# Gate products and last products of a gated unit as seven block products per pair of batches, with the operand places in another order

## The chip, the cores and the metric

The kernel runs on one core of one Trainium2 chip. The time is device microseconds of that core; each version is run several times, and its time is the median. The engines are PE (TensorE, matrix products), DVE (VectorE), ACT (ScalarE), POOL (GpSimd) and SP (SyncE, which starts the transfers). They run side by side, each through its own list of instructions, and wait for each other by semaphores. SBUF is the on-chip memory of 128 partitions; PSUM is the memory that PE writes, here eight banks of one result tile each.

## The reference

Attention, a mixing unit and a gated unit follow each other, all in float32, for 4 batches of 448 tokens and 768 features:

```
attn  = causal softmax(q k^T / 8) v                 # 4 batches, 12 heads, 448 tokens, 64 wide
x     = attn as [4, 448, 768]
u     = x + (relu(x^T w_tok1) w_tok2)^T             # over tokens, 448 -> 256 -> 448
u     = u + relu(u w_ch1) w_ch2                     # over features, 768 -> 1536 -> 768
h     = relu(u w_in)                                # 768 -> 1024
a, v  = h[..., :512], h[..., 512:]                  # gates, values
vn    = (v - mean(v)) / sqrt(var(v) + 1e-6)         # over the 512 features
vs    = w_spatial vn + b_spatial                    # over the 448 tokens
out   = (a * vs) w_out                              # 512 -> 768
```

## The kernel before

Every float32 operand x of a product is split into a high part (x rounded, written by ACT, `nc.scalar.copy`) and a low part (x minus the high part, written by DVE or POOL, `lo_part`), and a product takes three matmuls: high by high, high by low, low by high (`mm3`, lines L252 to L254). In names, `fb` and `fa` are such split factors of operands and weights, `whl` and `uhl` the same for plain products, `ghl` for the gated tiles, `gx` and `nhl` for normed values, `wv` for the value weights. A tile of the activations is feature-major: 128 features by 448 tokens; U0 to U3 hold the activations of the four batches.

The work: attention by pairs of heads (24 pairs), token mixing, then the mixing unit over features. Batches 0 and 1 take it by plain products (`channel`), batches 2 and 3 together (`channel_pair`): the two batches and two halves of the features make a matrix of two by two blocks, and so do the weights, and seven products of sums and differences of blocks stand for eight (`factors` and `weight_factors` make them, `seven` runs them; results `psf`, gathered into `hs` or added to U). Then the gated unit, batch by batch (`gate`): gate products (`psg`, 18 matmuls a tile, 4 tiles a batch), value products (`psv`, 18 matmuls of 512 columns), ACT's relu into one of two buffers `p0`, `p1`, the norm on DVE (L1141 to L1155, with a root on ACT between), spatial products (`psp`, 11 matmuls), on DVE the bias added and the gate multiplied, split into `ghl`, and the last products (`pso`, 12 matmuls a tile, 6 tiles a batch), copied to `gate` tiles and sent out.

All of this is declared as jobs of a planner (`Plan`) with priorities, what they read and write, and planned durations; it sets the order on each engine before the program is built, and gives each result the free bank of PSUM that became free last. Places in SBUF have names ("X", "A0", "h0", "st0", "P0") and are used one after another by different buffers. `EAGER, START, STEP` place the attention pairs in time.

## Time and profile before

| | us |
|---|---|
| median of 3 runs | 788.7 (788.41 to 789.03) |
| profiled execution | 789.54 |
| its span, first to last instruction | 787.8 |
| PE busy | 759.3 |
| PE weight loads busy | 651.9 |
| DVE busy | 541.5 |
| ACT busy | 394.7 |
| POOL busy | 314.0 |

The table gives the time in which each engine had an instruction under way. Matmuls overlap each other, so PE's busy time counts stretches and not the sum of the single durations. By the trace, the channel pair starts at about 416 us and the gated unit at about 562 us; the spatial products begin at about 690 us.

### The profile page before, as it was taken

The page shows a single profiled execution, that of the slowest core. Times are in us where ns is not written, and L with a number is a line of the kernel's source. Part 1 is how long each engine was busy: PE and PEld are TensorE (multiplying, and loading weights), DVE is VectorE, ACT ScalarE, POOL GpSimd, SP SyncE. Part 2 cuts the span into 40 slices and gives each one's busy share as a digit, 9 for nine tenths or more (in the row PEclk, how much of TensorE's full clock was granted, in tenths as well). Part 3 has the DMA queues.
Part 4 walks back from the last instruction along what each step waited for, and adds up shares of the span by engine and source line. Part 5 has one row for each costly group of instructions (what it writes and reads, how often), then busy time and mean ns, then how long its engine had stood idle before and what let it go on. Part 6 is the DMA issues. An engine that isn't in the chain of part 4 may idle for free.

```text
span 787.8 us, 12362 instructions
## 1 busy us (share of the span) xinstructions
PE 759.3 (96%) x4272; PEld 651.9 (83%) x4272; DVE 541.5 (69%) x1354; ACT 394.7 (50%) x977; POOL 314.0 (40%) x385
## 2 busy tenths in 40 slices
PE   5889899999999999999998999999999999999998
PEld 3467678788988788888897999989898898889997
DVE  5899888787777876775799679999601514383341
ACT  5999775627455664422445667453734323232110
POOL 4789645448766555643400000001797313031000
PEclk9999999999999999999999999999999999999999
DMA  7676687696857989888641221422321000001112
GB/s 260 216 239 235 210 296 237 222 350 225 290 163 224 302 282 284 255 261 267 195 151 41 85 78 39 156 105 74 101 88 48 1 1 0 1 1 70 71 47 93
DMA packets 49102, 123.32 MB, mean 157 GB/s; under 512 B 4880, under 2 KB 20368, under 8 KB 48528
## 3 DMA queue, kind: packets, MB, share of 16 engines
q1 hardware_dynamic: 49040, 122.54, 47.1%
q8 instruction: 33, 0.54, 0.3%
q14 instruction: 29, 0.24, 0.1%
HBM read 91.72 MB, written 30.80 MB: 156 GB/s over the span
## 4 chain that ended last, share of the span: by engine, by line
PE 71%; DVE 18%; ACT 5%; issue 2%; POOL 1%; DMA 1%; DVEq 0%; POOLq 0%; ACTq 0%
PE ps L252 7%; PE ps L254 7%; PE ps L253 7%; PE pss L400 4%; PE psf L252 4%; PE psf L253 4%; PE psf L254 4%; DVE fb L243 3%; PE pst L479 3%; PE pso L252 3%; PE pso L253 2%; PE pso L254 2%; PE psv L254 2%; PE psv L252 2%; PE psv L253 2%; PE psg L252 2%
## 5 line engine op out<-in xcount | busy, mean ns | idle before, releaser
L243 POOL TENSOR_TENSOR whl<-whl 128x768 fp32r<-128x768 f32 x45 | 83.7, 1862 | 82.5 <-ACT whl L718 81.4
L425 ACT ACTIVATE P<-P,stats 128x448 f32<-128x448 f32 (+1 forms) x192 | 95.9, 506 | 26.9 <-DVE stats L408 26.9
L442 POOL TENSOR_SCALAR P<-P,stats 128x448 f32<-128x448 f32 (+1 forms) x192 | 87.8, 477 | 51.2 <-DVE stats L434 34.0
L252 PE MATMUL psf<-fb,fa 128*128 128x448 f32 x252 | 93.2, 370 | 4.3 <-ACT uhl L724 1.7
L253 PE MATMUL psf<-fb,fa 128*128 128x448 f32 x252 | 92.9, 369 | 0.5 <-DVE fb L243 0.5
L254 PE MATMUL psf<-fb,fa 128*128 128x448 f32 x252 | 92.7, 368 | 0.0
L243 POOL TENSOR_TENSOR whl<-wf,whl 128x384 fp32r<-128x384 f32 x16 | 17.9, 1120 | 165.2 <-ACT whl L1054 165.2
L408 DVE CUSTOM_DVE_ANT_0 P<-pss,mask 128x448 f32<-128x448 f32 (+1 forms) x192 | 69.0, 412 | 14.1 <-PE pss L400 14.1
L1141 DVE BATCH_NORM_STATS2 bias<-v 128x6 f32<-128x512 f32 x14 | 9.7, 694 | 74.1 <-ACT v L1138 74.1
L855 ACT CAST fa<-raw 128x384 fp32r<-128x384 f32 x84 | 40.9, 511 | 39.0 <-PE psf L254 14.6
L718 ACT CAST whl<-whl 128x768 fp32r<-128x768 f32 x45 | 37.3, 832 | 43.9 <-DMA whl<-plain 41.9
L252 PEld LDWEIGHTS psf<-fb,fa 128*128 128x128 f32 x252 | 47.7, 189 | 10.4 <-issue 3.4
L252 PE MATMUL ps<-uhl,whl 128*128 128x448 f32 x144 | 55.0, 382 | 0.0
L252 PE MATMUL ps<-hid,whl 128*128 128x448 f32 x144 | 54.3, 377 | 0.4 <-DVE U L757 0.4
L254 PE MATMUL ps<-uhl,whl 128*128 128x448 f32 x144 | 52.8, 367 | 0.0
L254 PE MATMUL ps<-hid,whl 128*128 128x448 f32 x144 | 52.7, 366 | 0.0
L253 PE MATMUL ps<-uhl,whl 128*128 128x448 f32 x144 | 52.7, 366 | 0.0
L253 PE MATMUL ps<-hid,whl 128*128 128x448 f32 x144 | 52.7, 366 | 0.0
L253 PEld LDWEIGHTS psf<-fb,fa 128*128 128x128 f32 x252 | 47.8, 190 | 4.7 <-DVE fb L243 0.8
L243 DVE TENSOR_TENSOR fa<-raw,fa 128x384 fp32r<-128x384 f32 x84 | 46.8, 578 | 6.9 <-ACT fa L855 6.9
L254 PEld LDWEIGHTS psf<-fb,fa 128*128 128x128 f32 x252 | 47.8, 190 | 4.0
L243 POOL TENSOR_TENSOR uhl<-U,uhl 128x448 fp32r<-128x448 f32 x36 | 41.6, 1170 | 18.1 <-ACT uhl L1089 14.8
(175 smaller groups left out, 2037.4 us busy)
## 6 DMA issues: line engine op xcount, KB each, us to landing
way<-in_wch SPq DMA_DIRECT2D x24, 768.0 KB, 5.9
whl<-plain SPq DMA_DIRECT2D x45, 384.0 KB, 4.6
stage<-in_qkv SPq DMA_DIRECT2D x24, 448.0 KB, 4.6
plain<-way SPq DMA_DIRECT2D x24, 384.0 KB, 3.3
raw<-plain SPq DMA_DIRECT2D x24, 384.0 KB, 3.7
round<-PB SPq DMA_DIRECT2D x8, 1024.0 KB, 6.0
PT<-round SPq DMA_DIRECT2D x32, 256.0 KB, 6.2
v<-in_qkv SPq DMA_DIRECT2D x24, 256.0 KB, 3.5
```

The lines of the kernel that those rows point to most:

```text
L243: e.tensor_tensor(lo, x, hi.bitcast(F32), op=ALU.subtract)
L252: nc.tensor.matmul(ps, ah, bh, start=(first and i == 0), stop=False, **kw)
L253: nc.tensor.matmul(ps, ah, bl, start=False, stop=False, **kw)
L254: nc.tensor.matmul(ps, al, bh, start=False, stop=(last and i == n - 1), **kw)
L400: nc.tensor.matmul(ps(i, j), a.t[r, q0:q1], c.t[r, ks[j]], start=(k == 0), stop=(k == last))
L408: nc.vector.tensor_tensor_reduce(out=P(i)[:M, j, :], in0=ps(i, j), in1=mask[:M, S - 128 : S - 128 + W] if j == 0 and n < BLOCKS or M == 64 ...
L425: nc.scalar.activation(P(i)[:M, j, :], P(i)[:M, j, :], AF.Exp, bias=s.t[:M, 0, c : c + 1], scale=-1.0, accum_out=s.t[:M, 1, c : c + 1])
L442: nc.gpsimd.tensor_scalar(P(i)[:M, j, :], P(i)[:M, j, :], s.t[:M, 2, c : c + 1], 1.0, op0=ALU.mult, op1=ALU.mult)
L479: nc.tensor.transpose(ps.t[:, c : c + 128], src, ident)
L718: job("ACT", act(DM, False), lambda: nc.scalar.copy(w.t[:, 0, :], w.t[:, 1, :].bitcast(F32)), r=ks, w=ks, prio=p)
L855: nc.scalar.copy(w[o].t[:, z, 0], at(d))
L1141: nc.vector.bn_stats(sc(0, 6), v.t)
```

## The change

Gate products and last products are taken by pairs of batches (0 and 1, 2 and 3) as seven block products, like the channel pair. For a pair, `factors` makes the operand factors of the gate products from U, with an eighth place for the block b12, since the value products read the plain blocks of both batches; `gate_unit` makes the weight factors for one of two units; 252 instead of 288 matmuls. For the last products, the operand factors come from the gate tiles (`gated`), into which the spatial products now write, and the weight factors of all three units are made at once, 768 wide (`out_factors`); 252 instead of 288 matmuls, 6 to a block product. Results are gathered by ACT (copy, or activation) and by DVE (addition). Low parts of the gated unit's factors go to DVE (`GATE_DVE`, `OUT_DVE`, `NORMED_DVE`), the value weights stay with POOL and are loaded earlier, into other places. Further, the place X is two (X0, X1), `SETS` lists the places of the factors in another order, the first two factors of the channel pair have a higher priority (`EARLY`), and START and STEP are smaller.

```diff
-EAGER, START, STEP = 12, 115.0, 17.0
+EAGER, START, STEP = 12, 110.0, 16.7
...
+GATE_DVE = tuple(range(8))
+OUT_DVE = tuple(range(7))
...
+NORMED_DVE = (1, 2, 3)
+
+EARLY = 1e5 + 48
+VALUE_PRIO = -1e5 + 1.5
...
-    SETS = {2: ("h0", "h1", "h2"), 3: ("h3", "h4", "h5"), 4: ("qh0", "ql0", "qh1"), 5: ("A0", "A0", "v0"), 6: ("ql1", "st0", "st1"), 7: ("A1", "A1", "v1")}
...
+    SETS = (("qh0", "ql0", "qh1"), ("ql1", "st0", "st1"), ("A0", "A0", "v0"), ("A1", "A1", "v1"), ("h0", "h1", "h2"), ("h3", "h4", "h5"), ("X0",) * 3, ("X1",) * 3)
...
+    OVER = ((0, 0), (0, 0), (0, 1), (1, 0))
+
+    def factors(x, into, prio, place, on_dve=LO_DVE, early=None):
...
         def split(o, i, w):
             h, k, f = place[o][i]
             x_, wk = w
-            p = prio + 0.1 * o
+            p = (prio if early is None or o > 1 else early) + 0.1 * o
             job("ACT", act(S, False), lambda: nc.scalar.copy(f(0), x_()), r=wk, w=[(h, k, 0)], prio=p)
-            e, name, us = (nc.vector, "DVE", dve(S, False)) if o in LO_DVE else (nc.gpsimd, "POOL", pool(S))
+            e, name, us = (nc.vector, "DVE", dve(S, False)) if o in on_dve else (nc.gpsimd, "POOL", pool(S))
             job(name, us, lambda: lo_part(e, f(1), x_(), f(0)), r=[*wk, (h, k, 0)], w=[(h, k, 1)], prio=p, port=True)
...
-        for i in range(3):
+        for i in range(len(place[0])):
...
+            if len(place) > 7:
+                split(7, i, b12)
...
+    def split_weights(n, at, key, part, wkey, p, on_dve):
...
+        def split(o, d):
+            wk = wkey(o)
+            e, name, us_ = (nc.vector, "DVE", us) if o in on_dve else (nc.gpsimd, "POOL", pool(n))
+            job("ACT", act(n, False), lambda: nc.scalar.copy(part(o, 0), at(d)), r=[key(d)], w=[wk], prio=p + 0.1 * o)
+            job(name, us_, lambda: lo_part(e, part(o, 1), at(d), part(o, 0)), r=[key(d), wk], w=[wk], prio=p + 0.1 * o, port=True)
...
+    TO = ((0, 0), (0, 0), (1, 1), (0, 1), (0, 1), (1, 1), (1, 0))
+
+    def gather(o, ps, place, relu, prio):
+
+        h, hk = place(*TO[o])
+        if o in (0, 2, 3):
+            job("ACT", act(S), lambda: nc.scalar.copy(h(), ps.t[:, :S]), r=[(ps, 0)], w=hk, prio=prio)
+        elif o == 6:
+            job("ACT", act(S), lambda: nc.scalar.activation(h(), ps.t[:, :S], AF.Relu if relu else AF.Copy), r=[(ps, 0)], w=hk, prio=prio)
+        else:
+            job("DVE", dve(S), lambda: nc.vector.tensor_tensor(h(), ps.t[:, :S], h(), op=ALU.add), r=[*hk, (ps, 0)], w=hk, prio=prio)
+            if relu:
+                job("ACT", act(S, False), lambda: nc.scalar.activation(h(), h(), AF.Relu), r=hk, w=hk, prio=prio + 0.1)
...
+    def seven(us, place, base, done, start=()):
...
-                    mm3(ps.t[:, :S], [(w[o].t[:, z, 0, c], w[o].t[:, z, 1, c], place[o][i][2](0), place[o][i][2](1)) for i, c in enumerate((slice(0, 128), slice(128, 256), slice(256, 384)))], first=first, skip_group_check=True)
+                    w = us[z][0]
+                    mm3(ps.t[:, :S], [(w(o, 0, i), w(o, 1, i), place[o][i][2](0), place[o][i][2](1)) for i in range(n)], first=first, skip_group_check=True)
...
+                job("PE", 0.607 * n, mms, r=[*after, us[z][1](o), *((*place[o][i][:2], x) for i in range(n) for x in range(2))], w=[(ps, 0)], prio=base + 0.01 * o)
...
-            0,
+            places(*range(7)),
+            early=EARLY,
...
+        job("SP", 0.4, lambda k=k, w=w: nc.sync.dma_start(w.t, gated_w[8 + k]), r=[("gated", 8 + k)], w=[(w, 0)], prio=LOW + VALUE_PRIO + k, size=262144)
...
+        e, name, us = (nc.vector, "DVE", dve(FF, False)) if k in VALUE_DVE else (nc.gpsimd, "POOL", pool(FF))
+        job(name, us, lambda k=k, w=w, h=h, l=l, e=e: lo_part(e, l.t[:, k % 3, :], w.t, h.t[:, k % 3, :]), r=[(w, 0), (h, k, 0)], w=[(l, k, 1)], prio=LOW + VALUE_PRIO + k, port=True)
...
+    def gate_unit(f):
+
+        p = LOW + 110 + turn[0]
+        t, at, key = raw_blocks("w3", True)
+        for k in range(2):
+            for c in range(2):
+                job("SP", 0.4, lambda k=k, c=c: nc.sync.dma_start(t.t[:, k, c * HALF : c * HALF + HALF], gated_w[2 * f + 4 * k + c]), r=[("gated", 2 * f + 4 * k + c)], w=[(t, k, c)], prio=p, size=196608)
+        ws = [buf(tag, [2, 2, HALF], F32R, "fa") for tag in ("t0", "t1", "t2", "hid")]
+        split_weights(HALF, at, key, lambda o, x: ws[o // 2].t[:, o % 2, x], lambda o: (ws[o // 2], o % 2), p, GATE_DVE)
+        return lambda o, x, i: ws[o // 2].t[:, o % 2, x, 128 * i : 128 * i + 128], lambda o: (ws[o // 2], o % 2)
...
+    GATE_SETS = (5, 6, 7, 0, 1, 2, 3, 4), (6, 7, 0, 1, 5, 2, 3, 4)
...
+        place = factors(u_at, lambda k, i, u_at=u_at: u_at(*OVER[k], i), 1.0 + g, places(*GATE_SETS[g]), GATE_DVE)
+        dup = buf("e", [2, KM, 128], F32R, "xsh")
...
+        def hidden_pair(f, g=g, place=place):
+            if unit.get("f") != f:
+                unit.update(f=f, w=gate_unit(f))
+
+            def done(z, o, ps):
+                def at(r, x):
+                    h = gates[2 * g + x]
+                    return (lambda: h.t[:, 2 * r + f, :]), [(h, 2 * r + f)]
+
+                gather(o, ps, at, True, -1)
+
+            seven([unit["w"]], place, next_prio(), done)
+
+        if g == 0:
+            values(0)
+            hidden_pair(0)
+            values(1)
+            shared_values()
+            hidden_pair(1)
+        else:
+            hidden_pair(1)
+            values(0)
+            hidden_pair(0)
+            shared_values()
+            values(1)
...
+    gx = [buf(f"X{k}", [2, 2, FF], F32R, "gx") for k in range(2)]
...
+    def out_factors():
+
+        p0 = next_prio()
+        n = 2 * HALF
+        raws = [buf(f"A{k}", [2, n], F32, "raw") for k in range(2)]
+        more = buf("v1", [n], F32, "raw")
+        ws = [buf(t, [2, n], F32R, "fa") for t in ("hid", "t0", "t1", "t2", "P0", "P1", "x0")]
...
+        return [(lambda o, x, i, m=m: ws[o].t[:, x, HALF * i + 128 * m : HALF * i + 128 * m + 128], lambda o: (ws[o], 0)) for m in range(3)]
...
-            job("POOL", pool(FF), lambda c=c, x=x: lo_part(nc.gpsimd, ts[c - 1](1), x(), ts[c - 1](0)), r=[xk, tk[c - 1][0]], w=[tk[c - 1][1]], prio=p0)
+            e, name, us = (nc.vector, "DVE", dve(FF, False)) if c in NORMED_DVE else (nc.gpsimd, "POOL", pool(FF))
+            job(name, us, lambda c=c, x=x, e=e: lo_part(e, ts[c - 1](1), x(), ts[c - 1](0)), r=[xk, tk[c - 1][0]], w=[tk[c - 1][1]], prio=p0, port=True)
...
-            job("DVE", dve(S), lambda ps=ps, f=f: nc.vector.tensor_tensor(ps.t[:, :S], ps.t[:, :S], gates[b].t[:, f, :], op=ALU.mult), r=[p, (gates[b], f)], w=[p], prio=p0)
-            g = buf(("h0", "h1", "h2", "h3", "h4", "h5", "P0", "P1")[(4 * b + f) % 8], [2, S], F32R, "ghl")
-            job("ACT", act(S), lambda ps=ps, g=g: nc.scalar.copy(g.t[:, 0, :], ps.t[:, :S]), r=[p], w=[(g, 0)], prio=p0)
-            job("DVE", dve(S), lambda ps=ps, g=g: lo_part(nc.vector, g.t[:, 1, :], ps.t[:, :S], g.t[:, 0, :]), r=[p, (g, 0)], w=[(g, 1)], prio=p0)
...
+            job("DVE", dve(S), lambda ps=ps, f=f: nc.vector.tensor_tensor(gates[b].t[:, f, :], ps.t[:, :S], gates[b].t[:, f, :], op=ALU.mult), r=[p, gk], w=[gk], prio=p0)
...
+    def project(g, place, ws, units):
+        def done(z, o, ps):
+            def at(r, c):
+                i = 4 * (rows[0] + z) + 2 * r + c
+                h, k = gates[i % 8 // 2], 4 + i % 2
+                return (lambda: h.t[:, k, :]), [(h, k)]
+
+            gather(o, ps, at, False, -1)
+            if o in (1, 4, 5, 6):
+                (r, c), m = TO[o], units[z]
+                h, hk = at(r, c)
+                job("SP", 0.4, lambda: nc.sync.dma_start(out[2 * g + c, 128 * (m + 3 * r) : 128 * (m + 3 * r) + 128, :], h()), r=hk, prio=seq[0], size=229376)
+
+        seven([ws[m] for m in units], place, next_prio(), done)
+        rows[0] += len(units)
...
+    def gated(g, tags):
+        def at(r, c, i):
+            h = gates[2 * g + c]
+            return (lambda: h.t[:, 2 * r + i, :]), [(h, 2 * r + i)]
+
+        return factors(at, lambda k, i: at(*OVER[k], i), seq[0], pair_places(tags), OUT_DVE)
+
+    spatial(0, normed(0))
+    spatial(1, normed(1))
+    ws = out_factors()
+    place = gated(0, ("h0", "h1", "h2", "h3", "h4", "h5", "st0", "st1", "A0", "A0", "A1", "A1", "x1", "v1"))
+    spatial(2, normed(2))
+    project(0, place, ws, (0, 1))
+    ns = normed(3)
+    project(0, place, ws, (2,))
+    spatial(3, ns)
+    place = gated(1, ("X0", "X0", "X0", "X1", "X1", "X1", "w0", "w1", "h0", "h1", "h2", "h3", "h4", "h5"))
+    project(1, place, ws, (0,))
+    project(1, place, ws, (1, 2))
```

**In DVE's list of instructions, three places move.** At the start of the channel pair, between the second and the third gather of a result (`hs<-psf`); before:

```order
L948 TENSOR_TENSOR hs_4741<-psf_4787,hs_4741 128x448
L243 TENSOR_TENSOR fa_4843<-raw_4816,fa_4843 128x384
L875 TENSOR_TENSOR raw_4816<-raw_4816 128x384 x2
L875 TENSOR_TENSOR raw_4862<-raw_4816 128x384
L805 TENSOR_TENSOR hs_4741<-hs_4741 128x448
L243 TENSOR_TENSOR fb_4846<-ts_4841,fb_4846 128x448
L948 TENSOR_TENSOR hs_4818<-psf_4712,hs_4818 128x448
```

And of the change:

```order
L252 TENSOR_TENSOR fb_4816<-ts_4673,fb_4816 128x448
L815 TENSOR_TENSOR ts_4818<-U2_2593,ts_4662 128x448
L252 TENSOR_TENSOR fb_4831<-ts_4818,fb_4831 128x448
L815 TENSOR_TENSOR ts_4818<-U2_2593,ts_4662 128x448
L908 TENSOR_TENSOR hs_4775<-psf_4780,hs_4775 128x448
L252 TENSOR_TENSOR fb_4831<-ts_4818,fb_4831 128x448 x2
L908 TENSOR_TENSOR hs_4813<-psf_4747,hs_4813 128x448
L815 TENSOR_TENSOR hs_4775<-hs_4775 128x448
```

The part of a weight (`raw`, `fa`) that stood between these gathers has moved, and two factors stand there.

In the gated unit of batches 0 and 1, where norms of values follow each other (BN_STATS to vn; v are relu results, vn normed values); before:

```order
L1141 BN_STATS bias_3985<-v_6811 128x6
L1142 BN_AGGR bias_3985<-bias_3985 128x2
L1143 TENSOR_SCALAR bias_3985<-bias_3985 128x1
L1150 RECIPROCAL bias_3985<-bias_3985 128x1
L1152 TENSOR_SCALAR bias_3985<-bias_3985 128x1
L1153 TENSOR_SCALAR bias_3985<-bias_3985 128x1
L1154 TENSOR_SCALAR bias_3985<-bias_3985 128x1
L1155 TENSOR_SCALAR vn_6796<-v_6811,bias_3985 128x512
```

And of the change, at the norm of v_6388; psf_6391 and psf_6349 are gate products, gathered into the gate tiles of batch 1:

```order
L252 TENSOR_TENSOR fa_6441<-raw_6382,fa_6441 128x384
L252 TENSOR_TENSOR fa_6441<-raw_6439,fa_6441 128x384
L1108 RECIPROCAL bias_4002<-bias_4002 128x1
L1110 TENSOR_SCALAR bias_4002<-bias_4002 128x1
L1111 TENSOR_SCALAR bias_4002<-bias_4002 128x1
L1112 TENSOR_SCALAR bias_4002<-bias_4002 128x1
L1113 TENSOR_SCALAR vn_6460<-v_6388,bias_4002 128x512
L908 TENSOR_TENSOR gate1_6424<-psf_6391,gate1_6424 128x448
L908 TENSOR_TENSOR gate1_6424<-psf_6349,gate1_6424 128x448
```

Weight factors and gathers of gate products now stand between the two parts of a norm and behind it; PSUM bank 3, which psf_6391 holds, is that of the value product psv_6486 after it.

At the first spatial products (`psp`, whose eight products of batches 0 and 1 lie in banks 0, 7, 1, 0, 7, 1, 0, 7 before and 6, 5, 3, 5, 6, 5, 6, 5 after); before:

```order
L1225 TENSOR_TENSOR psp_7053<-psp_7053,bias_3985 128x448
L1226 TENSOR_TENSOR psp_7053<-psp_7053,gate0_6272 128x448
L243 TENSOR_TENSOR ghl_7094<-psp_7053,ghl_7094 128x448
L1225 TENSOR_TENSOR psp_7080<-psp_7080,bias_3985 128x448
L1226 TENSOR_TENSOR psp_7080<-psp_7080,gate0_6272 128x448
L243 TENSOR_TENSOR ghl_7111<-psp_7080,ghl_7111 128x448
```

And of the change, where raw_7040 and raw_7080 are blocks of the weights of the last products:

```order
L252 TENSOR_TENSOR fa_7212<-raw_7040,fa_7212 128x768
L1269 TENSOR_TENSOR psp_7198<-psp_7198,bias_4002 128x448
L1108 RECIPROCAL bias_4002<-bias_4002 128x1
L1110 TENSOR_SCALAR bias_4002<-bias_4002 128x1
L1111 TENSOR_SCALAR bias_4002<-bias_4002 128x1
L1112 TENSOR_SCALAR bias_4002<-bias_4002 128x1
L1113 TENSOR_SCALAR vn_7157<-v_7210,bias_4002 128x512
L1270 TENSOR_TENSOR gate0_6375<-psp_7198,gate0_6375 128x448
L252 TENSOR_TENSOR fa_7217<-raw_7040,fa_7217 128x768
L1269 TENSOR_TENSOR psp_7221<-psp_7221,bias_4002 128x448
L1270 TENSOR_TENSOR gate0_6375<-psp_7221,gate0_6375 128x448
L252 TENSOR_TENSOR fb_7243<-gate0_6375,fb_7243 128x448
```

Weight factors of 768 and the norm of a value stand among the additions and multiplications, the multiplication writes the gate tile, and an operand factor (`fb`) is made from it in place of `ghl`.

## Rows read from the trace of the kernel before

**Rows 1.** Page, engine totals: busy us, share, instructions.

```profile
PE 759.3 (96%) x4272; PEld 651.9 (83%) x4272; DVE 541.5 (69%) x1354; ACT 394.7 (50%) x977; POOL 314.0 (40%) x385
```

**Rows 2.** Stages: from:to, length, busy of PE, PEld, DVE, ACT, POOL; PE clock; DMA.

```profile
100.00:400.00 300.00, 298.44 (x1888) 254.68 (x1887) 230.86 (x596) 153.92 (x381) 163.41 (x169) 1.00 0.79 256
...
562.00:690.00 128.00, 127.27 (x597) 111.95 (x598) 37.04 (x115) 48.74 (x118) 61.16 (x74) 1.00 0.09 27
690.00:787.80 97.80, 92.71 (x454) 84.49 (x452) 39.77 (x67) 19.00 (x36) 8.13 (x7) 0.99 0.15 57
```

**Rows 3.** A group of PE by line: busy us, mean ns, idle before.

```profile
L252 PE MATMUL pso<-ghl,whl 128*128 128x448 f32 x96 | 35.2, 366 | 1.5 <-DVE ghl L243 1.5
```

**Rows 4.** Timeline of PE near the end: start, duration.

```profile
779.80 0.37 PE L252 MATMUL pso<-ghl,whl 128*128 128x448 f32 x1
...
783.85 0.37 PE L254 MATMUL pso<-ghl,whl 128*128 128x448 f32 x1
```

**Rows 5.** Waits of PE, 400 to 790 us: total, times, longest.

```profile
PE psf L252 <- ACT uhl L724: 1.7, 1, 1.7
PE psf L252 <- DVE hs L948: 1.6, 1, 1.6
PE pso L252 <- DVE ghl L243: 1.5, 1, 1.5
PE psg L252 <- ACT v L1138: 0.7, 1, 0.7
```

**Rows 6.** Timeline of PE at the channel pair's start.

```profile
424.17 0.37 PE L254 MATMUL psf<-fb,fa 128*128 128x448 f32 x1
426.19 0.44 PE L252 MATMUL psf<-fb,fa 128*128 128x448 f32 x1 [1.65 <-DVE hs L948]
...
428.23 0.74 PE L253 MATMUL psf<-fb,fa 128*128 128x448 f32 x1 [0.53 <-DVE fb L243]
...
431.38 0.41 PE L252 MATMUL psf<-fb,fa 128*128 128x448 f32 x1
```

**Rows 7.** Stretches at the channel pair's start, columns as in rows 2.

```profile
428.20:431.40 3.20, 3.17 (x9) 2.82 (x10) 3.17 (x7) 1.06 (x2) 0.00 (x0) 0.50 0.00 0
```

**Rows 8.** Timeline of DVE, back to back.

```profile
418.49 0.62 DVE L805 TENSOR_TENSOR ts<-U 128x448 f32<-128x448 f32 x1
...
420.09 0.62 DVE L243 TENSOR_TENSOR fb<-ts,fb 128x448 fp32r<-128x448 f32 x1
...
438.94 0.55 DVE L243 TENSOR_TENSOR fa<-raw,fa 128x384 fp32r<-128x384 f32 x1
...
439.88 0.62 DVE L948 TENSOR_TENSOR hs<-psf,hs 128x448 f32<-128x448 f32 x1
```

**Rows 9.** Timeline of DVE, the norm of a value.

```profile
676.34 0.69 DVE L1141 BATCH_NORM_STATS2 bias<-v 128x6 f32<-128x512 f32 x1 [11.52 <-ACT v L1138]
...
677.71 0.16 DVE L1150 RECIPROCAL bias<-bias 128x1 f32<-128x1 f32 x1 [0.27 <-ACT bias L1146]
...
678.66 0.55 DVE L1155 TENSOR_SCALAR vn<-v,bias 128x512 f32<-128x512 f32 x1
680.42 0.69 DVE L1141 BATCH_NORM_STATS2 bias<-v 128x6 f32<-128x512 f32 x1 [1.22 <-ACT v L1138]
```

**Rows 10.** Timeline of DVE, first spatial products.

```profile
691.42 0.62 DVE L1225 TENSOR_TENSOR psp<-psp,bias 128x448 f32<-128x448 f32 x1
...
693.31 0.63 DVE L243 TENSOR_TENSOR ghl<-psp,ghl 128x448 fp32r<-128x448 f32 x1 [0.60 <-ACT ghl L1228]
693.85 0.62 DVE L1225 TENSOR_TENSOR psp<-psp,bias 128x448 f32<-128x448 f32 x1
```

**Rows 11.** DVE and POOL at the same time, and a group of POOL.

```profile
380.07 4.33 DVE L243 TENSOR_TENSOR fb<-U,fb 128x448 fp32r<-128x448 f32 x2
379.90 6.19 POOL L243 TENSOR_TENSOR whl<-whl 128x768 fp32r<-128x768 f32 x3 [4.60 <-ACT whl L718]
L243 POOL TENSOR_TENSOR wv<-wf,wv 128x512 fp32r<-128x512 f32 x6 | 7.8, 1296 | 0.0
```

More of the change, by code (lines that the diff above doesn't have):

```diff
@@ L759, in channel @@
     def channel(b):
-        xs = buf("X", [KM, 2, S], F32R, "uhl")
+        xs = [buf(f"X{k}", [3, 2, S], F32R, "uhl") for k in range(2)]
         split_u(b, xs, -0.5)
@@ L826, in weight_factors, with raw_blocks, block, at @@
+    def raw_blocks(tag, rows):
+        t = buf(tag, [2, DM], F32, "raw")
+        t2 = buf(f"r{turn[0] % 2}", [HALF], F32, "raw")
+        turn[0] += 1
+        def block(d):
+            return d if rows else d[::-1]
+        def at(d):
+            if d is None:
+                return t2.t
+            k, x = block(d)
+            return t.t[:, k, x * HALF : x * HALF + HALF]
+        def key(d):
+            return (t2, 0) if d is None else (t, *block(d))
+        return t, at, key
     def weight_factors(us):
+        w = [buf(t, [2, 2, HALF], F32R, "fa") for t in WEIGHTS]
@@ L881, in weight_factors @@
-        return w
+            t, at, key = raw_blocks(f"w{turn[0] % 2}", rows)
+            for k, unit in enumerate((i, i2)):
+                job("SP", 0.4, lambda t=t, k=k, unit=unit: nc.sync.dma_start(t.t[:, k, :], plain[unit]), r=[("plain", unit)], w=[(t, k, x) for x in range(2)], prio=base + z, size=393216)
+            split_weights(HALF, at, key, lambda o, x, z=z: w[o].t[:, z, x], lambda o, z=z: (w[o], z), base + z, WEIGHT_LO_DVE)
+            made.append((lambda o, x, i_, z=z: w[o].t[:, z, x, 128 * i_ : 128 * i_ + 128], lambda o, z=z: (w[o], z)))
@@ L911, in seven @@
                     after += start
-                job("PE", 1.82, mms, r=[*after, (w[o], z), *((*place[o][i][:2], x) for i in range(3) for x in range(2))], w=[(ps, 0)], prio=base + 0.01 * o)
+                job("PE", 0.607 * n, mms, r=[*after, us[z][1](o), *((*place[o][i][:2], x) for i in range(n) for x in range(2))], w=[(ps, 0)], prio=base + 0.01 * o)
                 done(z, o, ps)
@@ L968, in channel_pair @@
             at = partial(h_at, q)
-            place = factors(at, lambda k, i, at=at: at(*((0, 0), (0, 0), (0, 1), (1, 0))[k], i), -0.5, 1 + q)
+            place = factors(at, lambda k, i, at=at: at(*OVER[k], i), -0.5, places(*((7 + 7 * q + o) % 8 for o in range(7))))
             for es in ((0,), (1, 2)):
@@ L1252, in mixer_kernel, with pair_places @@
-    ns = normed(0)
-    ready = spatial(0, ns)
-    for b in range(B):
-        if b + 1 < B:
-            ns = normed(b + 1)
-            following = spatial(b + 1, ns)
-        project(b, ready)
-        ready = following
+            job("DVE", dve(S), lambda ps=ps, f=f: nc.vector.tensor_tensor(gates[b].t[:, f, :], ps.t[:, :S], gates[b].t[:, f, :], op=ALU.mult), r=[p, gk], w=[gk], prio=p0)
+    def pair_places(tags):
+        flat = []
+        for t in dict.fromkeys(tags):
+            n = tags.count(t)
+            h = buf(t, [n, 2, S], F32R, "fb")
+            flat += [(h, i, lambda x, h=h, i=i: h.t[:, i, x, :]) for i in range(n)]
+        return [flat[2 * o : 2 * o + 2] for o in range(7)]
```

256 lines of the change are left out of this document (85 added, 171 removed).

## The prediction

> **What bounds the kernel now.** The first view is the page's line of engine totals [rows 1]: TensorE (PE) is busy 759.3 of 787.8 us, VectorE (DVE) 541.5. The profiled run took 789.54 us, 1.74 more than its span; the median of the runs shown, 788.7, lies 0.84 below it. All sums below are made against 789.54 and brought to the median by taking off 0.84. Then the table by stage [rows 2]: PE is full in every stage, 127.27 of 128 us at 562 to 690 and 92.71 of 97.8 at 690 to 787.8, while DVE is nearly full only up to 562. In the last 226 us, where most of the change lies, DVE has 37.04 + 39.77 = 76.8 us of work. So the last two stages are bound by PE alone, and what a removed matmul is worth is the spacing of matmuls. The busy mean of a 448-wide matmul is 366 ns, as in the group of the last products [rows 3], but they overlap: 20 of them start between 779.80 and 783.85 [rows 4], 0.2025 us each. That is the price of a matmul; 366 ns would nearly double the gain. The waits of PE after 400 us [rows 5] are few: 1.7, 1.6, 1.5 and 0.7 are the long ones. Nothing else can be won there.
>
> **The matmuls.** Gate products and last products go from 288 to 252 each, 72 fewer: 72 x 0.2025 = **-14.6**. Values and spatial products keep their number.
>
> **Old waits.** The wait of 1.7 (for ScalarE behind the splits of the gate's operand), the 0.7 ahead of a gate product and the 1.5 of the first last product for its high and low part [rows 5] hang on work that the change takes out: 1.7 + 0.7 + 1.5 = **-3.9**. Bounds: 0, if others come at the same places, which the new waits below count apart, and -3.9.
>
> **Start of the channel pair.** 14 matmuls lie between 424.17 and 431.38 [rows 6]: 7.21 us for 14 x 0.2025 = 2.84, so 4.4 us are lost. The first part is a wait of 1.65 for a gather of DVE; a stretch at half the clock follows, granted 0.50 of full speed, 1.2 instead of 2.4 GHz, after PE had stood idle with a few matmuls between [rows 7]. Eight matmul intervals there, 428.23 to 431.38, take 3.15 us instead of 1.62: a wait costs 1.5 more than itself when this happens. The change's other order of places and its early priority alter which DVE work stands ahead of that gather. In the order, two instructions instead of six lie between the second and the third gather, but weight factors that were ready before have moved ahead of the first. Bounds 0 and -4.4. I take half the wait, **-0.8**, because the number of DVE instructions around the place hardly falls.
>
> **What DVE gets.** Its order has 174 more instructions: 118 net of 448 elements, 33 of 384, 11 of 768, 12 of 512. Back to back the 448-wide cost 0.535 us (three intervals from 418.49 to 420.09) and the 384-wide 0.47 (two from 438.94 to 439.88) [rows 8]. No row has a 768-wide DVE operation; the step between those two prices, 0.065 per 64 elements, gives 0.86, two 384-wide give 0.94, and I take 0.87. The 512-wide lie between at 0.6. Sum: 63 + 15.5 + 9.6 + 7.2 = 95 us. In the last 226 us that makes 76.8 + 95 = 172, against about 211 of PE work (225.8 - 14.6), so DVE is not the bound on average. It queues, though: each instruction waits for those ahead of it, and PE waits where a bank of PSUM has not been read out.
>
> **Values and first gate products (new wait).** A norm on DVE takes 1.1 us (676.34 to the root, 677.71 less 0.27 idle), waits for ScalarE's root, and goes on for 1.5, from 677.71 to the end of the operation at 678.66 [rows 9]: 2.6 us. In the order after, the second part of the norm for v_6388 stands ahead of the gather gate1<-psf_6391, and the value product psv_6486 uses the same bank 3, so it can't start before. Count from the end of the last matmul of psf_5996, where both engines are abreast. DVE, to the gather: 0.4 for the result, 20 factor instructions of 0.535 = 10.7, then four norms (10.4), 19 instructions of 384 (9.0) and three of 448 (1.6): 32.1. PE, to psv_6486: 78 value matmuls at 0.227 (18 in the 4.08 us between the two norms of [rows 9]) = 17.7 and 54 at 0.2025 = 10.9: 28.6. PE waits **+3.5**. Bounds: 0 if DVE is a few instructions ahead at the start, 6 if every root is waited for too.
>
> **GpSimd beside DVE.** The value weights are split on GpSimd (six operations, 7.8 us) [rows 11], now in the tail of the channel pair, where DVE is busy with factors. At 380.07 two fb splits took 4.33 us, 2.16 each instead of 0.535, while GpSimd ran from 379.90 to 386.09 [rows 11]. Bounds 0 and +7.8; I take **+0.5**, since PE has its own work in that tail and 24 splits of U leave GpSimd altogether. The Trainium skill, SBUF — State Buffer, section Who interferes with whom, says that a DVE instruction with two SBUF inputs contends with a GpSimd instruction that reads SBUF, and that the loser blocks fully. The trace agrees, 2.16 beside 0.535; by the rule alone the whole 7.8 would stand on DVE, and the sum would end 7.3 higher.
>
> **Spatial products into last products (new wait).** Now an addition, a multiplication and, after 0.60 idle for ScalarE, a low part follow each spatial product [rows 10]: 2.43 us a block beside 11 matmuls x 0.2025 = 2.23. After, the low part is replaced, but three more things are in the queue: ten 768-wide operations on the weights of the last products, the last four norms, and the factors of the gate tiles. Count from the last matmul of psv_7030. DVE, until psp_7221 has been multiplied and its bank 5 is free: 0.7 for the relu, four norms 10.4, ten x 0.87 = 8.7, one normed part 0.6, two blocks of 1.25: 22.9. PE, until psp_7262 wants bank 5: 54 x 0.227 = 12.3 and three products of 2.23: 18.9. The wait is 4.0. From there to psp_7336, which wants bank 5 again, DVE has 9.7 (four factor splits and a difference 2.7, a weight 0.87, four blocks' pairs 5.0, two normed parts 1.2) and PE 8.9: 0.8 more. **+4.8**. Bounds: 0 and 8, if all of the chain's idle for ScalarE comes on top. The Trainium skill, Perfetto Trace Analysis, section Matmuls, says that independent groups of matmuls should rotate through different PSUM banks so that one's evacuation overlaps the next. Here the fourth product returns to the second's bank; by that rule a free fourth bank would give one product's 2.2 us back, and the wait would be 1.8.
>
> **Attention.** Its pairs are planned some 8 us earlier at the end (115 + 11 x 17 = 302, now 110 + 11 x 16.7 = 293.7). PE is busy 298.44 of 300 us there [rows 2], so no more than 1.6 can be won, and as much lost if two products move apart. I take 0.
>
> **Sum.** -14.6 - 3.9 - 0.8 + 3.5 + 0.5 + 4.8 = -10.5. 789.54 - 10.5 = 779.0, less 0.84: **778.2 us**.
>
> **Rivals.** *All new waits are hidden*: DVE is ahead when each stretch begins, since it has 211 - 172 = 39 us to spare. For it: splits that queue show little idle now. Against it: both counts above find DVE behind by more than one instruction. The sum is -19.3, the time 769.4.
> *DVE lags more than counted*: the second pair repeats the wait of 3.5, and two of the stalls bring the half clock, 1.5 each as at 428 us [rows 7]. 778.2 + 3.5 + 3.0 = 784.7. For it: norms and factors also meet in pair 1. Against it: there the values come last, with fewer weights to make.
> *Slower: DVE becomes the bound through the wait between high and low part*. Each of the 104 new pairs (ScalarE makes the high part, DVE the low part) could stand 0.60 us at the head of DVE's queue as the ghl pair does at 693.31 [rows 10]. 172 + 104 x 0.60 = 234 us for a stage that lasts 225.8 now: 8.6 longer, 797.3 at the median. It decides at (225.8 - 172) / 104 = 0.52 us a pair: above that, DVE alone needs longer than the stage takes now. Against it: splits that are queued several in a row follow each other at 0.535 without idle [rows 8], because ScalarE runs ahead.
> *Nothing gained*: new waits of 19 us in all eat the 19.3. No single stretch has that.
>
> **Chances.** Forecast 0.52 (its own range 775 to 782), hidden waits 0.20, more lag 0.18, slower 0.07, nothing 0.03. About 0.2%, 1.6 us, is what a measurement here can tell. Faster 0.90, same 0.03, slower 0.07. The range goes from the hidden case with attention's 1.4 (768) to the lagging case with 1.5 lost in attention (786); slower and nothing, 0.10, and the tails of the rest stay outside.
>
> **What would show it.** PE has 72 matmuls fewer (4200) and some 14 to 15 us less that lies between waits; DVE some 636 us busy. The waits name DVE's gather at the first value of batch 1's end (3 us) and DVE's gate multiplication at the fourth spatial product (4 us). The start of the channel pair still shows a stretch at half clock. If PE waits less than 3 us in the last 226 us, the hidden case is right; if ScalarE ends most of DVE's idle time there, and it is over 50 us, the slower one. The prediction is wrong in its sums if 768-wide operations take more than 0.94, or if a spatial product is held by something other than a bank.

## The result and the profile after

The changed kernel takes 780.75 us (median of 8 runs, 779.97 to 785.48), the kernel before 788.75 in the same comparison: ratio 0.991, 95% interval 0.9888 to 0.9931. That is 8.0 us less; 10.5 were forecast, with 768 to 786 as the range. The profiled execution took 780.77, its span 779.0, which is 8.8 less than the span before.

The page's engine totals, then three stages of the changed kernel (columns as in rows 2; the gated unit now begins at about 555 us, the spatial products at about 682):

```profile
PE 747.1 (96%) x4200; PEld 640.8 (82%) x4200; DVE 637.7 (82%) x1528; ACT 432.7 (56%) x1049; POOL 259.8 (33%) x333
```

```profile
100.00:400.00 300.00, 298.79 (x1897) 256.54 (x1896) 232.03 (x598) 153.85 (x381) 163.49 (x169) 1.00 0.80 255
555.00:680.00 125.00, 122.14 (x561) 105.63 (x560) 107.77 (x241) 68.86 (x159) 17.94 (x30) 0.99 0.14 42
680.00:779.00 99.00, 91.83 (x438) 83.92 (x436) 69.00 (x125) 35.66 (x67) 0.00 (x0) 0.97 0.15 56
```

Against [rows 1, 2]: 72 matmuls fewer, and DVE 637.7 us busy, where 541.5 + 95 = 636 had been worked out. DVE has 107.77 + 69.00 = 177 us of work in the last 224, up from 76.8. PE still has something under way nearly always, so what it lost must be read from its waits. All waits of PE from 400 us on, against [rows 5]:

```profile
PE psp L1262 <- DVE gate L1270: 3.3, 1, 3.3
PE psv L261 <- ACT v L1096: 2.7, 2, 2.4
PE psf L261 <- DVE hs L908: 1.6, 1, 1.6
PE psf L261 <- DVE U L767: 1.3, 1, 1.3
PE psf L261 <- ACT wv L1063: 1.3, 1, 1.3
PE psf L261 <- DVE U L987: 0.2, 1, 0.2
```

The old waits of 1.7, 0.7 and 1.5 are gone; four that [rows 5] doesn't have are there, the first two lines and the two of 1.3. A list of waits leaves out what the clock costs, so the starts of successive matmuls were compared with the usual distance between matmuls of their shape, and all that is longer was added up by place:

| us that PE loses, profiled runs | before | after |
|---|---|---|
| start of the channel pair | 4.6 | 3.9 |
| rest of the channel pair | 3.4 | 2.0 |
| values and gate products | 1.0 | 5.5 |
| spatial products and after | 2.3 | 6.1 |
| sum from 400 us | 11.3 | 17.5 |

17.5 - 11.3 = 6.2 more, -14.6 for the matmuls: -8.4. The remaining 0.4 of the span's -8.8 is the balance of small things: by 400 us PE had started 9 matmuls more (579 + 1897 against 579 + 1888), some 1.5 us, the tail behind the last one is 0.3 longer, and lengthenings too small for the table take back the rest.

**Start of the channel pair.** The 3.9 us here are other ones than the 4.6 before. The wait of 1.6 for a gather is as it was; a new wait for U stands ahead of it, with 1.5 us lost. The two short waits that followed before are gone, and so is the half clock of [rows 7]; the granted clock stays at 1.00 around the wait and behind it:

```profile
420.00:424.00 4.00, 2.43 (x13) 1.93 (x12) 4.00 (x9) 1.69 (x3) 0.00 (x0) 1.00 0.00 0
```

**Values.** First the timeline of PE in the changed kernel, then of ACT, then of DVE:

```profile
584.78 0.39 PE L263 MATMUL psv<-wv,fb 128*128 128x512 f32 x1
587.52 0.50 PE L261 MATMUL psv<-wv,fb 128*128 128x512 f32 x1 [2.36 <-ACT v L1096]
...
591.25 0.57 PE L263 MATMUL psf<-fb,fa 128*128 128x448 f32 x1
...
583.74 1.28 ACT L1104 ACT_TABLE_LOAD   x1
585.03 0.34 ACT L1104 ACTIVATE bias<-bias 128x1 f32<-128x1 f32 x2
586.87 0.60 ACT L1096 ACTIVATE v<-psv 128x512 f32<-128x512 f32 x1 [1.50 <-DVE vn L1113]
...
580.81 1.73 DVE L252 TENSOR_TENSOR fb<-U,fb 128x448 fp32r<-128x448 f32 x3
...
583.04 0.68 DVE L1099 BATCH_NORM_STATS2 bias<-v 128x6 f32<-128x512 f32 x1
...
586.21 0.55 DVE L1113 TENSOR_SCALAR vn<-v,bias 128x512 f32<-128x512 f32 x1
```

The first norm starts on DVE only at 583.04, behind the operand factors. The third value's relu waits for one of the two relu buffers, which the first norm frees at 586.76, and the fifth value product waits for the bank that this relu reads. Behind it matmuls of 448 columns take 0.57 instead of 0.36 us until about 592 us, at a granted clock of 0.51; that makes 1.7 us beside the wait:

```profile
588.50:591.70 3.20, 3.20 (x10) 2.69 (x10) 3.17 (x7) 1.89 (x4) 0.00 (x0) 0.51 0.00 0
```

**Spatial products.** Timeline of DVE, then PE, then the stretches around them:

```profile
689.38 0.62 DVE L1270 TENSOR_TENSOR gate<-psp,gate 128x448 f32<-128x448 f32 x1
689.91 0.95 DVE L252 TENSOR_TENSOR fa<-raw,fa 128x768 fp32r<-128x768 f32 x1
690.78 0.63 DVE L1269 TENSOR_TENSOR psp<-psp,bias 128x448 f32<-128x448 f32 x1
691.44 0.62 DVE L1270 TENSOR_TENSOR gate<-psp,gate 128x448 f32<-128x448 f32 x1
...
692.12 0.74 PE L1262 MATMUL psp<-wsp,gx 128*128 128x448 f32 x1 [3.25 <-DVE gate L1270]
```

```profile
688.50:692.00 3.50, 0.37 (x2) 0.00 (x0) 3.39 (x8) 0.56 (x1) 0.00 (x0) 0.85 0.00 0
692.00:694.00 2.00, 1.88 (x5) 1.71 (x6) 2.00 (x4) 0.57 (x1) 0.00 (x0) 0.50 0.00 0
694.00:697.50 3.50, 3.50 (x10) 3.08 (x10) 2.00 (x5) 2.12 (x4) 0.00 (x0) 0.50 0.00 0
```

The fourth product starts at 692.12, right behind the second one's multiplication (691.44 + 0.62), as forecast. After it the granted clock is 0.50, 1.2 GHz, for 5.5 us: the wait costs 3.4, the clock another 2.7.

### The profile page after: what moved, and what is told of

Read it like the earlier page. It is cut to its first block, busy times and chain, and to the rows that moved or that the text cites. A ratio compares the mean times of both kernels' runs of the same rounds, so it can differ in the third digit from the quotient of the medians.

```text
span 779.0 us, 12423 instructions
## 1 busy us (share of the span) xinstructions
PE 747.1 (96%) x4200; PEld 640.8 (82%) x4200; DVE 637.7 (82%) x1528; ACT 432.7 (56%) x1049; POOL 259.8 (33%) x333
## 4 chain that ended last, share of the span: by engine, by line
PE 61%; DVE 27%; ACT 6%; issue 3%; DMA 2%; POOL 1%; DVEq 0%; ACTq 0%; POOLq 0%; SPq 0%
PE ps L261 7%; PE ps L263 7%; PE ps L262 7%; DVE fb L252 6%; PE psf L261 5%; PE psf L263 5%; PE psf L262 5%; DVE fa L252 4%; PE pss L409 4%; DVE raw L859 3%; PE pst L488 3%; DVE U L987 2%; PE pso L578 2%; ACT P L434 2%; DVE U L815 2%
## 5 line engine op out<-in xcount | busy, mean ns | idle before, releaser
L261 PE MATMUL psf<-fb,fa 128*128 128x448 f32 x420 | 154.7, 368 | 4.4 <-DVE hs L908 1.6
L263 PE MATMUL psf<-fb,fa 128*128 128x448 f32 x420 | 154.0, 367 | 0.0
L262 PE MATMUL psf<-fb,fa 128*128 128x448 f32 x420 | 154.0, 367 | 0.0
L261 PEld LDWEIGHTS psf<-fb,fa 128*128 128x128 f32 x420 | 79.3, 189 | 13.4 <-issue 1.9
L262 PEld LDWEIGHTS psf<-fb,fa 128*128 128x128 f32 x420 | 79.3, 189 | 6.7
L263 PEld LDWEIGHTS psf<-fb,fa 128*128 128x128 f32 x420 | 79.2, 189 | 6.8 <-DVE fa L252 0.2
L846 ACT CAST fa<-raw 128x384 fp32r<-128x384 f32 (+1 forms) x112 | 57.0, 531 | 41.4 <-DVE raw L859 18.4
L252 DVE TENSOR_TENSOR fa<-raw,fa 128x384 fp32r<-128x384 f32 (+1 forms) x112 | 65.5, 611 | 9.8 <-ACT fa L846 9.6
L252 POOL TENSOR_TENSOR wv<-wf,wv 128x512 fp32r<-128x512 f32 x6 | 8.5, 1430 | 161.0 <-DVE fb L252 153.1
L810 ACT CAST fb<-U 128x448 fp32r<-128x448 f32 x57 | 30.2, 566 | 29.5 <-DVE U L815 12.2
L488 PE MATMUL pst<-ident,P 128*128 128x128 f32 x256 | 38.7, 287 | 5.7 <-POOL P L451 4.5
```

Of the source, the lines that this page charges most:

```text
L252: e.tensor_tensor(lo, x, hi.bitcast(F32), op=ALU.subtract)
L261: nc.tensor.matmul(ps, ah, bh, start=(first and i == 0), stop=False, **kw)
L262: nc.tensor.matmul(ps, ah, bl, start=False, stop=False, **kw)
L263: nc.tensor.matmul(ps, al, bh, start=False, stop=(last and i == n - 1), **kw)
L488: nc.tensor.transpose(ps.t[:, c : c + 128], src, ident)
L810: job("ACT", act(S, False), lambda: nc.scalar.copy(f(0), x_()), r=wk, w=[(h, k, 0)], prio=p)
```

## The experiments

The theory after this reading: PE loses what DVE's queue is late with, and each such wait costs again through the clock. The rivals name the buffer or bank at which the wait shows, the blocking between GpSimd and DVE, or other parts of the change. Each edit is made to the changed kernel unless said otherwise. Ratios are against the kernel before; the changed kernel's is 0.991 (0.9888 to 0.9931).

**A third relu buffer.**

```diff
-        v = buf(f"p{turns[0] % 2}", [FF], F32, "v")
+        v = buf(("p0", "p1", "sh1")[turns[0] % 3] if turns[0] < 7 else f"p{turns[0] % 2}", [FF], F32, "v")
```

> Change: the values of batches 0 and 1 rotate over three relu buffers instead of two, so a relu no longer waits until the norm before last is done. Baseline of the changed kernel: 780.8 us, with 2.4 us of waiting and 1.7 us at half clock between 584 and 592 us. Theory A (the buffer is what makes PE wait there): the wait and the half clock go, 4.1 us less, about 776.7. Theory B (DVE's queue is behind as a whole in this stretch, the buffer is only where it shows first): DVE has no idle time between 571 and 605 us, the gather of psf_6391 still ends at the same time, and PE waits at psv_6486 instead, about 3.5 to 4 us; 779 to 781.

780.32 us, 0.9878 (0.9847 to 0.9909): no clear difference. The waits of PE from 570 to 610 us in this run:

```profile
PE psv L261 <- DVE gate L908: 1.5, 1, 1.5
PE psv L261 <- ACT v L1096: 1.0, 1, 1.0
PE psf L261 <- ACT gate L904: 0.6, 1, 0.6
```

The 2.4 became 1.0, and 1.5 turned up at the gather of psf_6391, the place that the prediction had named. The waits add up to nearly the same. B: the buffer is only where DVE's lateness shows first. No half clock follows these shorter waits, and still the run takes 115.84 us from the first value product to the first spatial product, the changed kernel 115.81.

**Low parts of the last products' weights on GpSimd.**

```diff
             p0,
-            OUT_DVE,
+            (),
         )
```

> Change: the low parts of the seven 768-wide weight factors of the last products are made by GpSimd instead of DVE. Baseline 780.8 with 3.3 us of waiting and 2.7 us at half clock between 688 and 698 us. Theory A (DVE's queue ahead of the second spatial product's multiplication causes the wait): six of the low parts, 6 x 0.87 = 5.2 us, leave that queue, wait and half clock go, about 775. Theory B (GpSimd and DVE block each other when both read SBUF): seven operations of about 1.9 us, 13 us, stand in DVE's way, the wait stays or grows; 780 to 786.

779.51 us, 0.9862 (0.9829 to 0.9894), no clear difference; PE still waits 2.6 at the fourth spatial product. DVE, then GpSimd, in this run:

```profile
683.15 1.78 DVE L1113 TENSOR_SCALAR vn<-v,bias 128x512 f32<-128x512 f32 x1
...
688.48 2.18 DVE L1113 TENSOR_SCALAR vn<-v,bias 128x512 f32<-128x512 f32 x1
...
681.00 3.65 POOL L252 TENSOR_TENSOR fa<-raw,fa 128x768 fp32r<-128x768 f32 x2 [4.03 <-ACT fa L846]
686.74 5.59 POOL L252 TENSOR_TENSOR fa<-raw,fa 128x768 fp32r<-128x768 f32 x3 [2.10 <-ACT fa L846]
```

The norm's last operation, 0.55 alone, takes 1.78 and 2.18 beside GpSimd. The work left DVE, and most of the room was lost to blocking (with a third norm 3.4 of the 5.2 us): B, though the wait shrank by 0.7 and did not grow.

Ahead of the edit's place the run is a repeat of the changed kernel, and it shows what the half clock among the values is worth. The wait at the fifth value product is 2.4 again, but the granted clock stays at 1.00. PE then waits at psv_6486 for the gather that the prediction had named; first that product, then the stretch up to it:

```profile
605.18 0.50 PE L261 MATMUL psv<-wv,fb 128*128 128x512 f32 x1 [1.04 <-DVE gate L908]
```

```profile
590.00:606.00 16.00, 14.96 (x71) 12.82 (x70) 14.98 (x40) 7.14 (x16) 0.00 (x0) 1.00 0.17 50
```

From the first value product to the first spatial product it takes 115.72 us, against 115.81 with half clock. So DVE's queue sets how long this stage lasts, and the 1.7 us of half clock only stand where a later wait would.

**The bank that has been free longest, for spatial products.**

```diff
-                    b.tag = min(b.banks, key=lambda i: (bank_free[i] > s, -bank_free[i] if bank_free[i] <= s else bank_free[i]))
+                    b.tag = min(b.banks, key=lambda i: (bank_free[i] > s, -bank_free[i] if bank_free[i] <= s and not b.oldest else bank_free[i]))
...
             ps = bank(everything, "psp")
+            ps.oldest = True
```

> Change: each spatial product takes the PSUM bank that has been free longest, not the one that became free last; nothing else. Theory A (the wait of 3.3 us at the fourth spatial product is one for its bank): the eight products of batches 0 and 1 run without a wait, the half clock behind it goes too, about 775. Theory B (DVE's queue is the bound of the stretch whatever the banks): the wait returns at the first last products, whose operand factors come from the same queue; 778 to 781.

776.28 us, 0.9829 (0.9803 to 0.9855), clearly faster than the changed kernel. The eight products run without a wait. What is left of waits from 660 us on:

```profile
PE psf L262 <- DVE fb L252: 0.4, 1, 0.4
PE psf L261 <- ACT gate L904: 0.3, 1, 0.3
PE psf L261 <- DVE gate L1271: 0.2, 1, 0.2
```

A for the most part. With B's place, the first last products, some 1.7 us of loss remain, so of the 3.4 us of waiting and 2.7 of half clock 4.5 came back. DVE, ACT and POOL have the same order as in the changed kernel.

**Extra matmuls in the place of the wait.** 16 matmuls that the output doesn't use:

```diff
+            if b == 0 and f == 2:
+                fill(16, tk, p0 + 0.25)
```

> Change: 16 matmuls of 448 columns into a bank that nobody reads are put ahead of the fourth spatial product, 3.2 us of work at the place where PE waits 3.3 us; they are of no use for the output. Theory A (the half clock behind the wait follows from PE's standing still): the granted clock stays at 1.00 from 688 to 698 us and 2.7 us come back, about 778. Theory B (the clock falls there for another reason): no gain, 781 to 784, if the extra matmuls are not hidden.

779.1 us, 0.9871 (0.9837 to 0.9905): 1.65 us less by the medians, within the intervals, so the trace decides. The profiled execution is the quickest of four; its span is 776.4 for 779.0. The same two stretches:

```profile
688.50:692.00 3.50, 3.49 (x18) 2.91 (x17) 3.47 (x7) 1.14 (x2) 0.00 (x0) 1.00 0.00 0
692.00:697.50 5.50, 5.50 (x29) 5.10 (x28) 5.39 (x9) 3.12 (x6) 0.00 (x0) 1.00 0.00 0
```

PE did useless work as long as it had waited, and the clock stayed at 1.00. From the first spatial product to the last matmul the run takes 90.81 us for 92.69: 1.9 of the span's 2.6 us come from here, and the other 0.7 lie ahead of it. A: with PE kept busy the clock doesn't fall here. Of the 2.7 us 1.9 come back, because 0.7 of new waits follow at about 700 us.

**START and STEP as before.**

```diff
-EAGER, START, STEP = 12, 110.0, 16.7
+EAGER, START, STEP = 12, 115.0, 17.0
```

> Change: START and STEP are 115 and 17.0 again, all else as in the changed kernel (780.8 us). Theory A (the attention pairs' times are worth nothing, as forecast): 779 to 782, and the time that PE loses between 100 and 400 us stays within 1 us. Theory B (they gave the 2.3 us by which the lost time between 100 and 400 us is lower in the changed kernel): about 783.

786.32 us, 0.9958 (0.9938 to 0.9978): 5.6 us slower, more than either theory had. PE starts 1867 matmuls between 100 and 400 us, not 1897; the loss is spread, without one large wait.

From the first value product on, PE, DVE and ACT have the order of the changed kernel, so the run also repeats the wait at the fourth spatial product. PE there, then the stretch behind it:

```profile
699.70 0.47 PE L1262 MATMUL psp<-wsp,gx 128*128 128x448 f32 x1 [3.25 <-DVE gate L1270]
```

```profile
700.00:706.00 6.00, 6.00 (x31) 5.57 (x30) 5.87 (x11) 3.36 (x7) 0.00 (x0) 1.00 0.00 0
```

The same wait of 3.25 is followed by the full clock, and this stage takes 90.79 us for 92.69, as with the extra matmuls. In three other runs with this wait (a third relu buffer, without the early factors, value weights planned on DVE) half clock cost some 1.6 behind it, where the profiled run of the changed kernel had 2.7. So the wait alone doesn't decide whether the clock falls; what does stays open.

**The two constants in the kernel before.**

```diff
-EAGER, START, STEP = 12, 115.0, 17.0
+EAGER, START, STEP = 12, 110.0, 16.7
```

> Change: the kernel before with START and STEP of the change (110 and 16.7), nothing else. Putting the old values into the changed kernel cost 5.5 us. Theory A (the two constants are a gain by themselves, whatever else is in the plan): 783 to 784. Theory B (they only suit the changed plan): 788 to 791.

789.1 us, 0.9991 (0.9971 to 1.0011). B: alone they are worth nothing that can be told from noise (0.9 us by the medians). What they are worth, they are worth in the changed plan.

**Without the early factors.**

```diff
             places(*range(7)),
-            early=EARLY,
```

> Change: the first two factors of the channel pair have their old priority, the order of places stays new. Lost PE time at the start of the channel pair is 4.6 us before the change and 3.9 after. Theory A (the early factors are what won this): 0.7 us more, about 781.5. Theory B (the order of places did, or neither): 780 to 781, and without the early factors the start is the same within 0.3 us.

781.21 us, 0.9888 (0.9853 to 0.9923). PE loses 1.5, 0.4, 1.8 and 0.4 us at the start of the channel pair, as with them. B.

**Only the gate products in the new form.** Spatial and last products are those of the kernel before (the functions from there), their weights in A0, A1, t0, t1.

```diff
-    ws = out_factors()
-    place = gated(0, ("h0", "h1", "h2", "h3", "h4", "h5", "st0", "st1", "A0", "A0", "A1", "A1", "x1", "v1"))
+    out_w = [buf(t, [2, DM], F32R, "whl") for t in ("A0", "A1", "t0", "t1")]
```

> Change: only the gate products are taken as seven block products; spatial products, their splits and the last products are as before (36 more matmuls, weights of the last products split on GpSimd, normed low parts on GpSimd). Theory A (the last products' new form gains its 36 matmuls, 7.3 us, and pays 6.1 us of waiting and half clock at the spatial products, where the old form lost 2.2): 780.8 + 7.3 - 6.1 + 2.2 = 784.2. Theory B (the two halves gain the same, and the waits at the spatial products come from the gated unit's backlog whatever the last products are): 788, with a wait at the fourth spatial product still there.

783.87 us, 0.9931 (0.9903 to 0.9958). A: no wait at the fourth spatial product, the old 1.5 for ghl is back, and the last products' new form is worth 3.1 us net of its 7.3 by the medians, whose intervals overlap.

**Value weights' low parts planned on DVE.**

```diff
-VALUE_DVE = ()
+VALUE_DVE = tuple(range(6))
```

> Change: the low parts of the value weights are made by DVE, not GpSimd. Theory A (the 1.5 us lost at 546 us come from GpSimd's wv operations blocking two splits on DVE, which take 3.11 us there): that wait goes, 779.3. Theory B (DVE is full at the end of the channel pair, 143.9 of 155 us, so six operations of 0.6 us more on it are worse than the blocking): 782 to 784.

789.24 us, 1.0009 (0.9991 to 1.0027): all that the change had won is gone. One wait of PE:

```profile
PE psf L263 <- DVE fa L252: 13.1, 1, 13.1
```

The plan put gate products ahead of the values, and PE had nothing else while DVE made the rest of their factors. Both theories missed this; for their question the run is void.

**The norm's true length in the plan.**

```diff
-        job("DVE", 0.8, first, r=[(v, 0)], w=[st], prio=p0)
+        job("DVE", 1.1, first, r=[(v, 0)], w=[st], prio=p0)
...
-        job("DVE", 0.65, second, r=[st, (v, 0)], w=[st, dkey], prio=p0)
+        job("DVE", 1.5, second, r=[st, (v, 0)], w=[st, dkey], prio=p0)
```

> Change: the planner is told what a norm takes on DVE (1.1 and 1.5 us for its two parts instead of 0.8 and 0.65); the work is the same, the order of the gated unit is drawn up anew. Theory A (the waits at 585 and 688 us come from a plan that thinks DVE free earlier than it is): a plan with the true durations puts other work there, and most of the 4.2 and 6.1 us go, about 773 to 777. Theory B (DVE has too much to do between 571 and 605 us in any order): the first of them stays somewhere, 777 to 781.

771.04 us (771.00 to 772.33), 0.9775 (0.9748 to 0.9803): 9.7 less than the changed kernel, with the same work. The waits of PE from 400 us on:

```profile
PE psf L261 <- DVE U L987: 1.8, 2, 1.6
PE psf L261 <- DVE hs L908: 1.6, 1, 1.6
PE psf L261 <- DVE U L767: 1.3, 1, 1.3
PE psf L261 <- ACT v L1096: 1.2, 1, 1.2
PE psv L261 <- DVE U L987: 0.2, 1, 0.2
```

The wait at the spatial products is gone, that at the values is 1.2, and PE loses 2.2 us there instead of 5.5. DVE's list has weight factors behind the spatial products' additions and multiplications where they stood ahead of them:

```profile
683.59 0.62 DVE L1269 TENSOR_TENSOR psp<-psp,bias 128x448 f32<-128x448 f32 x1
684.25 0.62 DVE L1270 TENSOR_TENSOR gate<-psp,gate 128x448 f32<-128x448 f32 x1
684.79 0.62 DVE L252 TENSOR_TENSOR fb<-gate,fb 128x448 fp32r<-128x448 f32 x1
685.33 0.95 DVE L252 TENSOR_TENSOR fa<-raw,fa 128x768 fp32r<-128x768 f32 x1
```

A, beyond its range. Up to 585 us DVE and ACT have the order of the changed kernel, and behind it the same amount of DVE's work, in another order, goes without these waits. Banks are given out anew too, so this run alone doesn't part order from banks; the next one keeps both.

**A shorter norm.** Without the refinement of the reciprocal root:

```diff
-            nc.vector.tensor_scalar(t, r, r, sc(8), op0=ALU.mult, op1=ALU.mult)
-            nc.vector.tensor_scalar(t, t, -0.5, 1.5, op0=ALU.mult, op1=ALU.add)
-            nc.vector.tensor_scalar_mul(r, r, t)
```

> Change: the three small DVE operations that refine the reciprocal root in each of the 14 norms are left out, so the norm's factor is the plain reciprocal of the root; each norm is 0.75 us shorter on DVE, the order and the banks stay. Theory A (the length of DVE's queue sets both waits): one norm stands ahead of the first wait and four ahead of the second, 2.4 becomes 1.6 and 3.3 becomes 0.3, and the half clock behind the second goes; 780.8 - 0.8 - 3.0 - 2.7 = 774. Theory B (buffers and banks set them, whatever DVE's load): less than 1 us, 780 to 781.

771.86 us, 0.9782 (0.9755 to 0.9809): 8.9 less. The wait at the values is 1.6, that at the spatial products 0.6 in two pieces. Behind both the granted clock stays at 1.00. ACT's order is that of the changed kernel, and DVE's list lacks only the left-out operations. A: DVE's queue sets both.

**Value weights on DVE in GpSimd's places**, on top of the norm's true length; the orders of the other engines are untouched:

```diff
-        job(name, us, lambda k=k, w=w, h=h, l=l, e=e: lo_part(e, l.t[:, k % 3, :], w.t, h.t[:, k % 3, :]), r=[(w, 0), (h, k, 0)], w=[(l, k, 1)], prio=LOW + VALUE_PRIO + k, port=True)
+        job(name, us, lambda k=k, w=w, h=h, l=l, e=nc.vector: lo_part(e, l.t[:, k % 3, :], w.t, h.t[:, k % 3, :]), r=[(w, 0), (h, k, 0)], w=[(l, k, 1)], prio=LOW + VALUE_PRIO + k, port=True)
```

> Change: on top of the norm's true durations in the plan (771.0 us), the six low parts of the value weights are made by DVE at the very places where the plan has them on GpSimd; the orders of PE, ScalarE and the transfers stay word for word the same. Theory A (GpSimd blocks DVE there: the splits beside the six wv operations take 5.8 us longer than alone, while six operations on DVE would be 3.6 us): DVE gets 2 us back, the 1.8 us that PE loses at 545 us mostly go, about 769.5. Theory B (that loss has nothing to do with GpSimd, and DVE is full there): no gain, 771 to 774.

769.88 us (6 runs), 0.9733 (0.9706 to 0.976); the step from 0.9775 is within the intervals, and the trace decides. First the changed kernel's DVE and GpSimd, then DVE in this run:

```profile
542.83 3.11 DVE L252 TENSOR_TENSOR fb<-hs,fb 128x448 fp32r<-128x448 f32 x2
...
542.53 2.92 POOL L252 TENSOR_TENSOR wv<-wf,wv 128x512 fp32r<-128x512 f32 x2 [153.12 <-DVE fb L252]
```

```profile
543.28 1.15 DVE L252 TENSOR_TENSOR fb<-hs,fb 128x448 fp32r<-128x448 f32 x2
...
544.88 0.68 DVE L252 TENSOR_TENSOR wv<-wf,wv 128x512 fp32r<-128x512 f32 x1
```

Two splits take 1.15 instead of 3.11, and the 1.8 us that PE lost at 545 us are gone. A. This is the fastest version here, ahead of both kernels.

## Why the prediction was right, and where it was not

The direction, the bound and most of the places held; the gain came out 2.5 us too high. By stages against the table, PE lost 1.7 us more among the values than forecast and 0.5 more at the spatial products; the rest came out within 0.2. By its steps:

- **Matmuls, -14.6.** 72 fewer. Their usual distance is unchanged, 0.203 us; no run isolates the term.
- **Old waits, -3.9.** The three are gone.
- **Start of the channel pair, -0.8.** 4.6 became 3.9 (the forecast's 4.4 took 13 distances between 14 matmuls for 14). The size is right by luck: the wait of which half was to go is still there at 1.6, the half clock that was to stay is gone, and a new wait took 1.5 us. The early factors have no part in it, and whether the order of places has was not tried.
- **What DVE gets, 95 us.** 96.2 measured. A 768-wide operation takes 0.87 from start to start (689.91 to 690.78), the value taken.
- **Values, +3.5.** 5.5 measured in this stage. The cause, DVE's queue ahead of psv_6486, holds. This is the term that was mis-sized most: 4.5 us more are lost than before, where 3.5 less the old wait of 0.7, 2.8, were forecast. The wait came one product earlier, because the count left out that relu and norm share two buffers. It brought 1.7 us of half clock, which the sum didn't have, but these are no loss of their own: without them PE waits at psv_6486 instead, and either way 4.2 us go between 584 and 606 us. The other 1.3 are small waits, 0.6 of them in the second pair.
- **GpSimd beside DVE, +0.5.** Mis-sized: 1.5 at 546 us. The Trainium skill's rule that the prediction cited (SBUF — State Buffer, Who interferes with whom) holds here: two splits took 3.11 beside GpSimd and 1.15 without it. Its 7.8 as a whole on PE would have been too much.
- **Spatial products, +4.8.** 6.1 measured: 3.4 of waiting, where 4.0 and 0.8 were counted, and 2.7 of half clock. The first wait is 0.6 shorter and the second didn't come; the clock was left to the rival of more lag. A stall was priced as the stall alone, though [rows 6, 7] showed one that cost more. The waits, counted 1.4 too high, hid half of that, so the near hit here is luck in part: where the clock stayed up, this stage took 1.9 us less.
- **The rule on rotating banks** (the Trainium skill, Perfetto Trace Analysis, Matmuls) was put at 2.2 us; taking the oldest bank gave 4.5, because the whole wait and the half clock went, and 1.7 came back at the last products.
- **Attention, 0.** Right within the noise for the two constants alone (0.9991). In the changed kernel PE comes to its 2507th matmul at 406.81 us instead of 408.27, inside the bound of 1.6, and loses as much in the new wait for U. With the old values the changed plan takes 5.6 more, so they belong to the change; why, stays open.
- **The rivals.** DVE's wait between high and low part did not decide: 28 fb splits of the gate tiles stood idle 0.7 us in all. The repetition in the second pair is 0.6, not 3.5. Hidden waits are what the plan with the true norm came near, at 771.0 for 769.4. The rival of more lag saw the half clock, at a price that the stages bear out only at the spatial products.
